# Two output accumulators in one PSUM bank, and the bank left over keeps a quarter of a V chunk

## The chip, the cores and the metric

The kernel runs on one core of a Trainium2 chip. Its time is the device time in microseconds (us), the median of several runs. A profile is one more execution, recorded by the hardware profiler, and it has its own time: the span from its first to its last instruction, and around the span a little that the span does not see.

The core has five engines, each with an instruction queue of its own that is worked off in order: TensorE (PE; its weight loads are shown as PEld), VectorE (DVE), ScalarE (ACT), GpSimd (POOL) and SyncE (SP), which here issues nearly all DMA transfers. SBUF is the working memory of 128 partitions. PSUM is the memory that TensorE writes its products to; it has eight banks, each 128 partitions by 512 float32.

## The reference, cut to what matters

The reference is two layers of decoding with one new position for each of 8 batch rows: attention over a cache, then a mixer with an MLP, and both once again. The caches are the same in both passes. (Lines are shortened; with a sequence of one position the shift brings in zeros alone, so `hs` is 0 and the kernel leaves it out.)

```python
B, Sq, D = 8, 1, 448
Hq, Hkv, Sk, Dh = 16, 8, 4096, 256        # k_cache, v_cache: (B, Hkv, Sk, Dh), bfloat16
...
def _A_ref(x, k_cache, v_cache, wq, wo):
    q = (x @ wq) split into Hq heads
    scores = einsum("bhqd,bhkd->bhqk", q, k) * (Dh ** -0.5)
    p = _softmax(scores, axis=-1)
    o = einsum("bhqk,bhkd->bhqd", p, v)
    return o as (B, Sq, Hq * Dh) @ wo

def _B_ref(x, w1, w2, w3, w4):
    hs = (h shifted along the sequence by quarters) @ w2   # h = _gelu(_layernorm(x) @ w1)
    x1 = x + hs
    return x1 + _gelu(_layernorm(x1) @ w3) @ w4
...
x = x + _A_ref(_layernorm(x, axis=-1), A_k_cache, A_v_cache, A_wq, A_wo)
x = x + _B_ref(_layernorm(x, axis=-1), B_w1, B_w2, B_w3, B_w4)
x = x + _A_ref(_layernorm(x, axis=-1), A_k_cache, A_v_cache, A_wq, A_wo)
x = x + _B_ref(_layernorm(x, axis=-1), B_w1, B_w2, B_w3, B_w4)
```

K and V of one batch row are 32 MiB together, 256 MiB for all rows, and each of the two attention passes needs all of them. What is computed per byte is little: two query heads share a K/V head.

## The kernel before

**Tiles.** The work of a row is cut into four pairs of K/V heads (`gp` 0 to 3). The K of a pair and the V of a pair are four *chunks* each, of 128 partitions x 8 KiB = 1 MiB. A chunk `c` of a pair is an *item* `(n, kv, c)`; `n` is the task (pass `ps`, row `b`, pair `gp`), `kv` is 0 for K and 1 for V. SBUF has 15 *places* of one chunk each (`slots`, `NC = 15`). Every item is loaded into a free place, used, and the place is given back.

**What stays between the passes.** Pass 1 of a row starts when pass 0 and the MLP of that row are done; meanwhile other rows' chunks are loaded. Eleven chunks of each row stay in their places from pass 0 to pass 1 and are not loaded again (`kept`: all K chunks of pairs 3 and 2, and V chunks 1 to 3 of pair 3). One more, `inner` (V chunk 1 of pair 2), stays in PSUM: `away` copies it with four transposes of 128x512 32-bit words into the four banks `store` (L719), and `back` copies it from there into a place before it is used in pass 1 (L726). A VectorE transpose turns blocks, and doing it twice gives the data back. So a row loads 52 of its 64 chunks from HBM.

**Order.** `items` fixes the order of work once and for all: the four K chunks of a task, with the V chunks of the task before it in between. The main loop takes one item after the other. After each item `emit_loads` issues every load for which a place is free, in the order of `loads`; all go through SP's one queue, so a load that waits for its place holds up those behind it. Two K chunks in neighbouring places can be loaded by one DMA of 2 MiB (L647). In the stretch in which a row's kept chunks lie in their places, only four of the 15 are left for the stream.

**A K chunk** is transposed in place by three VectorE instructions (`transpose_k`, L684), then TensorE makes scores into the bank `sc` (L699), ScalarE takes exponentials (L708), and the probabilities are transposed by TensorE (L735) and copied to `ptw` (L742). **A V chunk** takes 16 products of 128x256 (`pv`, L754), four in each quarter of the accumulator's partitions. Two pairs (a *half*, `g8`) add into one accumulator; there are two accumulators, `o_banks`, each in a PSUM bank of its own, of which the first 256 columns are used. The first four products of a half start the sums anew (`start=`, kept track of in `begun`), the others add.

**The end of a half** (`half`) is made in steps that the main loop spreads between items: VectorE takes the sums of exponentials (L398, L401), TensorE adds them up (L409), VectorE makes `rz` and `R` (L412, L429), ScalarE copies the accumulator to SBUF (L435) and the accumulator is free for the next half (`in_use`); at the next step TensorE multiplies the copy by `R` (L440) and VectorE casts the result (L444). This happens 31 times: 16 halves in pass 0, 15 in pass 1; the last row's first half of pass 1 is computed another way (`pv_cols`), in two of the `store` banks.

**PSUM.** The eight banks are `misc`, `sc`, two `o`, four `store`.

Of the kernel before, what the change touches and what calls it, by code (L numbers as in the profile page):

```python
# [8 lines left out]
FP32 = mybir.dt.float32  # L9
BF16 = mybir.dt.bfloat16  # L10
U32 = mybir.dt.uint32
# [6 lines left out]
def kernel(  # L18
# [27 lines left out]
    nc = tc.nc  # L46
# [3 lines left out]
    Dh = A_k_cache.shape[3]  # L50
# [5 lines left out]
    GP = G // 2  # L56
# [6 lines left out]
    kept = [(gp, 0, n) for gp in (GP - 1, GP - 2) for n in range(4)]  # L63
    kept += [(GP - 1, 1, n) for n in range(1, 4)]
    inner = (GP - 2, 1, 1)

    consts = ctx.enter_context(tc.tile_pool(name="consts", bufs=1))
    work = ctx.enter_context(tc.tile_pool(name="work", bufs=2))
    chn = ctx.enter_context(tc.tile_pool(name="chn", bufs=1))
    psum = ctx.enter_context(tc.tile_pool(name="psum", bufs=1, space=bass.MemoryType.PSUM))  # L70
# [4 lines left out]
    slots = [places_t[:, n * PB : (n + 1) * PB] for n in range(NC)]  # L75
# [32 lines left out]
    ptz = consts.tile([128, 520], BF16, name="ptw")  # L108
# [3 lines left out]
    misc = psum.tile([128, 512], FP32, name="misc")  # L112
    ot_bank = misc[:, 256:320]
    sc = psum.tile([128, 512], FP32, name="sc")
    o_banks = [psum.tile([128, 512], FP32, name=f"o{n}") for n in range(2)]
    store = [psum.tile([128, 512], FP32, name=f"store{n}") for n in range(4)]
    for t in [sc] + o_banks:
        nc.vector.memset(t[:], 0.0)

    def room_ps(what, nb):  # L120

# [301 lines left out]
    def half(o_ps, zall, g8, OT):  # L423


        rz = yield from z_cols(zall, range(2 * g8, 2 * g8 + 2))

        R = chn.tile([128, 8], FP32, tag="R")
        nc.vector.tensor_mul(  # L429
            R[:].rearrange("p (g n) -> p g n", n=4),  # L430
            rz[:].rearrange("p n g -> p g n"),
            fold[:].rearrange("p (g n) -> p g n", n=4),
        )
        o_sb = chn.tile([128, Dh], FP32, tag="o_sb")
        nc.scalar.copy(o_sb[:], o_ps[:, 0:Dh])  # L435
        in_use.remove(o_ps)
        yield
        ot_ps = ot_bank[:, 32 * g8 : 32 * g8 + 16].rearrange("p (j h) -> p j h", j=2)
        for j in range(2):
            nc.tensor.matmul(  # L440
                ot_ps[:, j], o_sb[:].rearrange("p (i j) -> p j i", j=2)[:, j], R[:], start=True, stop=True
            )
        yield
        nc.vector.tensor_copy(OT[:, :, 8 * g8 : 8 * g8 + 8], ot_ps)  # L444
        yield

    in_use = []
# [41 lines left out]
    def last(b, st):  # L489
        yield from half(st["o", 0], st["z"], 0, OT2[:, :, :, b])  # L490
# [13 lines left out]
    tasks = [(0, 0, gp) for gp in free + keep] + [(0, 1, gp) for gp in free]  # L504
# [26 lines left out]
    items, due = [], []  # L531
# [10 lines left out]
    def stays(it):  # L542
        n, kv, c = it
        return (tasks[n][2], kv, c) in kept

    def inside(it):
        n, kv, c = it
        return (tasks[n][2], kv, c) == inner

    loads = [it for it in items if not (tasks[it[0]][0] == 1 and (stays(it) or inside(it)))]  # L550

# [2 lines left out]
    where = {}  # L554
# [69 lines left out]
    def taken(it, p):  # L624

        where[it] = p
        n, kv, c = it
        if stays(it):
            where[tasks[n][1:], it[1:]] = p
        free_at[p] = again[tasks[n][1:], kv, c] if tasks[n][0] == 0 and stays(it) else used_at[it]  # L630

    def emit_loads(most=None):
        n = 0
        while loads and places and n != most:
            it = loads[0]
            both = both_for(it)
            if both:
                p, mate = both
                if p not in places or p + 1 not in places:
                    break  # L640
                for i, q in ((it, p), (mate, p + 1)):
                    loads.remove(i)
                    places.remove(q)
                    del held[i]
                    taken(i, q)
                _, b, gp = tasks[it[0]]
                nc.sync.dma_start(  # L647
                    places_t[:, p * PB : (p + 2) * PB],
                    A_k_cache[b, 2 * gp : 2 * gp + 2]
                    .rearrange("g s d -> (g s) d")  # L650
                    .rearrange("(p u z) d -> u p (z d)", u=2, z=32)[it[2] // 2],
                )
                n += 1
                continue
            p = place_for(it)
            if p is None:
                break
            del loads[0]
            taken(it, p)
            t, kv, c = it  # L660
            _, b, gp = tasks[t]
            dst = slots[p]
            rows = (A_v_cache if kv else A_k_cache)[b, 2 * gp : 2 * gp + 2].rearrange(
                "g s d -> (g s) d"
            )
            if kv:
                src = rows.rearrange("(a p y) d -> a p (y d)", a=4, y=16)[c]
            else:
                src = rows.rearrange("(p x y) d -> x p (y d)", x=4, y=16)[c]
            if loads:  # L670
                nc.sync.dma_start(dst[:], src)
            else:
                for y in range(2):
                    nc.sync.dma_start(
                        dst[:, 8 * Dh * y : 8 * Dh * (y + 1)], src[:, 8 * Dh * y : 8 * Dh * (y + 1)]
                    )
            n += 1
# [38 lines left out]
    def away(slot):  # L716

        for n in range(4):
            nc.vector.transpose(  # L719
                store[n][:].bitcast(U32), slot[:].bitcast(U32)[:, 512 * n : 512 * n + 512]  # L720
            )
# [22 lines left out]
            pt_ps.rearrange("p t k (a h) -> p a (t k) h", a=4),  # L744
        )

    def pv(o_ps, v, a, gp, begin):


        g = 2 * gp + a // 2  # L750
        for y in range(16):
            q = y % 4
            at = 128 * a + 8 * (4 * q + y // 4) + 6 - 2 * (g % 4)
            nc.tensor.matmul(  # L754
                o_ps[32 * q : 32 * q + 8, 0:256],
                ptz[:, at : at + 8],
                v[:, y * Dh : (y + 1) * Dh],
                start=(begin and y < 4),
                stop=(y >= 12),
                skip_group_check=True,  # L760
            )
# [39 lines left out]
            except StopIteration as e:  # L801
                return e.value

    gens, pairs_done, p_of, begun = [], {}, {}, set()

    def add_gen(kind, b, g, at, until, total):
        gens.append({"kind": kind, "b": b, "g": g, "at": at, "until": until, "n": 0, "of": total})
# [22 lines left out]
    for idx, it in enumerate(items):  # L830
# [7 lines left out]
        n, kv, c = it  # L838
        ps, b, gp = tasks[n]
# [5 lines left out]
        slot = slots[p]  # L845
        final = (ps, b) == (1, Bn - 1)
        if kv == 0:
# [6 lines left out]
            st = state[ps, b]  # L854
# [41 lines left out]
        else:  # L896
            st = state[ps, b]
# [5 lines left out]
            if final and gp in free:  # L903
                pv_cols(oc, slot, c, gp)
                if c % 2 == 1:

                    u = c // 2
                    scale_o(oc, rz_gp, gp, u, OT2[:, :, :, b])
                    h0 = 8 * gp + 4 * u
                    run(  # L910
                        add_cols(
                            st["y"],
                            lambda i: OT2[:, i % 2, i // 2, MID:],
                            wo_sb,
                            range(h0, h0 + 4),
                            4,
                            open=(claim(st), gp == free[-1] and u == 1),
                        )
                    )
            else:  # L920
                g8 = gp // 2
                if ("o", g8) not in st:
                    while len(in_use) == 2:
                        step(10 * len(items))
                    st["o", g8] = next(t for t in o_banks if all(t is not u for u in in_use))
                    in_use.append(st["o", g8])
                pv(st["o", g8], slot, c, gp, begin=(ps, b, g8) not in begun)
                begun.add((ps, b, g8))
                if ps == 0 and inside(it):
                    away(slot)  # L930
            if c == 3:
                done = pairs_done[ps, b] = pairs_done.get((ps, b), 0) + 1
                if done == 2 and ps == 0:
                    add_gen("chain", b, first_half(b, st), idx + 1, idx + (16 if b == 0 else 21), 10)
                elif done == 2:
                    add_gen("chain" if final else "last", b, first_last(b, st), idx + 1, idx + 13, 9)
                elif done == 4 and ps == 0:
                    add_gen("chain", b, chain(b, st), idx + 1, first_of[(1, b), 0] - 1, 38)
                elif done == 4 and not final:
                    add_gen("last", b, last(b, st), idx + 1, idx + (7 if b == Bn - 2 else 13), 6)  # L940
        if not (ps == 0 and stays(it)):
            if (ps, gp, kv, c) == (1, keep[-1], 0, 0):
                kept_place = p
            else:
                places.append(p)
        emit_loads()
        step(idx)
    while gens:
# [6 lines left out]
    for q in range(4):  # L955
        for fc in range(4):
            at = min(128 * fc, D - 128)
            lo, hi = max(W * q, 128 * fc), min(W * q + W, at + 128)
            if lo < hi:
# [4 lines left out]
                    start=(lo == W * q),  # L964
                    stop=False,
                    skip_group_check=True,
                )
    for c in range(HC):
        for q in range(4):
# [4 lines left out]
                start=False,  # L974
                stop=(c == HC - 1),
# [38 lines left out]
```

## Time and profile before

| | |
|---|---|
| median of 5 runs | 1104.07 us (1101.73 to 1109.72) |
| the profiled execution | 1105.06 us, of which the span is 1103.1 |
| TensorE busy / weight loads | 677.1 us (61%) / 453.0 us (41%) |
| VectorE busy | 586.3 us (53%) |
| ScalarE busy | 124.5 us (11%) |
| read from HBM | 446.77 MB, 405 GB/s over the span |
| granted TensorE clock, mean | 0.589 of full speed |

The page gives for each group of instructions its line, engine and operation, what it writes and reads, its count, then after the bar its busy time and the mean of one in ns, then the idle time of the engine before it and what ended most of that. The groups around the change:

```profile
L684 DVE STREAM_TRANSPOSE places<-places 128x512 uint32<-128x512 uint32 (+1 forms) x576 | 462.1, 858 | 279.6 <-DMA places<-in_A_k_cache_dram 276.5
...
L754 PE MATMUL o<-places,ptw 128*8 128x256 bf16 x3968 | 244.1, 390 | 138.1 <-DMA places<-in_A_v_cache_dram 128.7
```

VectorE's largest group waits for K chunks from HBM, and TensorE's products with V wait for V chunks. The section of DMA issues has line, number, size, and the median time from issue to landing:

```profile
places<-in_A_v_cache_dram SPq DMA_DIRECT2D x223, 1024.0 KB, 9.5
places<-in_A_k_cache_dram SPq DMA_DIRECT2D x146, 1024.0 KB, 10.3
places<-in_A_k_cache_dram SPq DMA_DIRECT2D x23, 2048.0 KB, 19.7
```

### The profile page before, as it was taken

What the parts mean: (1) busy time and instruction counts of PE and PEld (TensorE: products, weight loads), DVE (VectorE), ACT (ScalarE), POOL (GpSimd) and SP (SyncE); (2) the same over time, 40 slices, a digit from 0 to 9 for tenths busy, and PEclk for the clock granted to TensorE, in tenths of its full rate; (3) what the DMA queues carried; (4) which work ended last, traced back from release to release, by engine and by line L of the source; (5) the groups of instructions that cost most, each with busy time, mean ns of one, the idle gap of its engine ahead of it and who ended that gap; (6) DMA issues with size and microseconds to landing.
All of it is one profiled execution on the core that took longest, in us unless ns stands there. A gap on an engine that the chain in (4) does not pass through costs nothing. (4 is left out here: it accounts for less than half of the span.)

```text
span 1103.1 us, 32833 instructions
## 1 busy us (share of the span) xinstructions
PE 677.1 (61%) x15062; PEld 453.0 (41%) x15062; DVE 586.3 (53%) x1188; ACT 124.5 (11%) x362; POOL 16.3 (1%) x27
## 2 busy tenths in 40 slices
PE   3245677556864577446774467735776477767775
PEld 2123345334642355324542245523454244535554
DVE  4255564646356555455455564565637563575462
ACT  0001101110110011101011000201111101111110
POOL 0000000000000000000000000000000000000000
PEclk9996556655565556555566555765556555665575
DMA  9999999999999999999999999999999999999994
GB/s 359 395 425 420 419 403 416 419 412 406 416 423 421 394 390 424 423 418 388 419 420 424 420 398 419 423 422 417 411 416 421 419 405 420 420 411 404 414 418 182
DMA packets 62011, 448.90 MB, mean 407 GB/s; under 512 B 6569, under 2 KB 10545, under 8 KB 11313
## 3 DMA queue, kind: packets, MB, share of 16 engines
q1 hardware_dynamic: 61680, 446.42, 98.4%
q8 instruction: 118, 1.93, 0.7%
q10 hardware_dynamic: 192, 0.38, 0.1%
q14 instruction: 21, 0.16, 0.0%
HBM read 446.77 MB, written 0.01 MB: 405 GB/s over the span
## 5 line engine op out<-in xcount | busy, mean ns | idle before, releaser
L684 DVE STREAM_TRANSPOSE places<-places 128x512 uint32<-128x512 uint32 (+1 forms) x576 | 462.1, 858 | 279.6 <-DMA places<-in_A_k_cache_dram 276.5
L699 PE MATMUL sc<-places,qbd 128*8 128x128 bf16 (+1 forms) x6720 | 283.7, 310 | 227.6 <-DVE places L684 188.9
L754 PE MATMUL o<-places,ptw 128*8 128x256 bf16 x3968 | 244.1, 390 | 138.1 <-DMA places<-in_A_v_cache_dram 128.7
L699 PEld LDWEIGHTS <-qbd 128*8 128x8 bf16 x6720 | 162.8, 102 | 324.9 <-issue 148.1
L754 PEld LDWEIGHTS <-ptw 128*8 128x8 bf16 x3968 | 113.0, 110 | 185.1 <-issue 142.9
L708 ACT ACTIVATE p_n<-sc 128x256 bf16<-128x256 f32 x128 | 95.7, 748 | 808.1 <-PE sc L699 808.1
L287 PEld LDWEIGHTS <-wq_sb 128*128 128x128 bf16 x1152 | 36.0, 104 | 28.6 <-issue 18.9
L336 PEld LDWEIGHTS <-wo_sb 128*128 128x128 bf16 x1280 | 38.5, 102 | 19.6 <-issue 19.4
L310 DVE CAST qbd<-misc 32x64 bf16<-32x64 f32 x64 | 13.8, 216 | 61.3 <-PE misc L306 60.7
L287 PE MATMUL misc<-xb,wq_sb 128*128 128x1 bf16 x1024 | 34.6, 166 | 6.7 <-DVE xb L262 3.3
L336 PE MATMUL misc<-OT,wo_sb 128*128 128x1 bf16 x1024 | 34.4, 165 | 0.0
L708 ACT ACTIVATION_READ_ACCUMULATOR p_n<-sc 128x1 f32 x128 | 34.3, 268 | 0.0
L742 ACT CAST ptw<-misc 128x128 bf16<-128x128 f32 x64 | 17.5, 273 | 136.8 <-PE misc L735 76.7
L440 PEld LDWEIGHTS misc<-R,o_sb 128*128 128x128 f32 x124 | 27.1, 303 | 10.4 <-issue 8.3
L440 PE MATMUL misc<-R,o_sb 128*128 128x8 f32 x124 | 29.8, 351 | 0.4 <-ACT o_sb L435 0.3
L237 POOL TENSOR_TENSOR t<-t,nhalf 128x2 f32<-128x2 f32 (+2 forms) x20 | 14.0, 703 | 1073.6 <-DVE t L251 1073.6
L409 PE MATMUL misc<-zm,one 128*128 128x8 f32 (+1 forms) x66 | 18.3, 351 | 16.2 <-DVE zm L401 14.4
L726 DVE STREAM_TRANSPOSE places<-store 128x512 uint32<-128x512 uint32 x32 | 20.1, 685 | 11.3 <-PE sc L699 11.3
L409 PEld LDWEIGHTS misc<-zm,one 128*128 128x128 f32 x66 | 15.7, 296 | 22.4 <-issue 17.1
L354 PEld LDWEIGHTS <-w_sb 128*128 128x128 bf16 x560 | 17.2, 105 | 9.6 <-issue 9.4
L354 PE MATMUL misc<-xb,w_sb 128*128 128x1 bf16 (+1 forms) x560 | 18.4, 166 | 3.6 <-DVE xb L264 2.2
L719 DVE STREAM_TRANSPOSE store<-places 128x512 uint32<-128x512 uint32 x32 | 20.0, 694 | 1.0 <-DMA places<-in_A_v_cache_dram 0.9
(93 smaller groups left out, 227.2 us busy)
## 6 DMA issues: line engine op xcount, KB each, us to landing
places<-in_A_v_cache_dram SPq DMA_DIRECT2D x223, 1024.0 KB, 9.5
places<-in_A_k_cache_dram SPq DMA_DIRECT2D x146, 1024.0 KB, 10.3
places<-in_A_k_cache_dram SPq DMA_DIRECT2D x23, 2048.0 KB, 19.7
wo_sb<-in_A_wo_dram SPq DMA_DIRECT2D x1, 3584.0 KB, 27.0
wq_sb<-in_A_wq_dram SPq DMA_DIRECT2D x3, 1024.0 KB, 8.5
w_sb<-in_B_w_dram SPq DMA_DIRECT2D x1, 1568.0 KB
w_sb<-in_B_w_dram SPq DMA_DIRECT2D x3, 448.0 KB, 25.7
places<-in_A_v_cache_dram SPq DMA_DIRECT2D x2, 512.0 KB, 18.7
```

The source lines that it names most:

```text
L287: nc.tensor.matmul(q_ps[:, j * Hq + h, :], w, xbs(nb)[:, xi, :], start=(fc == 0), stop=(fc == 3),)
L336: nc.tensor.matmul(y_ps[:, fc, :], w[:, i, at : at + 128], rhs(i), start=start, stop=stop, skip_group_check=open is not None,)
L354: nc.tensor.matmul(h_ps[:, c * nb : c * nb + nb], w, xbs(nb)[:, xi, :], start=(fc == 0), stop=(fc == 3),)
L409: nc.tensor.matmul(z_ps, ones, zm[:], start=True, stop=True)
L440: nc.tensor.matmul(ot_ps[:, j], o_sb[:].rearrange("p (i j) -> p j i", j=2)[:, j], R[:], start=True, stop=True)
L684: nc.vector.transpose(w, w)
L699: nc.tensor.matmul(sc[32 * k : 32 * k + 8, 128 * x : 128 * (x + nx)], qbd[:, ep, gp].rearrange("p a h -> p (a h)"), v, start=(n == 0), sto ...
L708: nc.scalar.activation(p_sb[:, :, :, 2 * u : 2 * u + 2].rearrange("p t i x -> p x t i"), sc[:, 256 * u : 256 * u + 256].rearrange("p (x t ...
L719: nc.vector.transpose(store[n][:].bitcast(U32), slot[:].bitcast(U32)[:, 512 * n : 512 * n + 512])
L726: nc.vector.transpose(slot[:].bitcast(U32)[:, 512 * n : 512 * n + 512], store[n][:].bitcast(U32))
L742: nc.scalar.copy(ptw[:, :, :, 6:8], pt_ps.rearrange("p t k (a h) -> p a (t k) h", a=4),)
L754: nc.tensor.matmul(o_ps[32 * q : 32 * q + 8, 0:256], ptz[:, at : at + 8], v[:, y * Dh : (y + 1) * Dh], start=(begin and y < 4), stop=(y >= ...
```

## The change

The two accumulators become the two halves of one bank, `o_both`: columns 0 to 255 and 256 to 511. One TensorE product of zeros (128x512) at the start sets the whole bank; from then on no product starts a sum anew (`start=False`), and the half of the bank that ScalarE has just copied out is set to zero by VectorE (`memset`, 128x256), 31 times. `begun` goes.

The bank left over becomes `store[4]`. In pass 0, after the products with V chunk 0 of pair 3 (`part`), VectorE transposes the first quarter of that chunk (`Q4` = 4 x 256 columns, 128x512 32-bit words) into it. In pass 1 the load of this chunk brings only the other three quarters, 128 x 6 KiB, and VectorE transposes the first quarter from PSUM into the chunk's place. This instruction is issued at the end of the item just before the chunk's own. That is done once per row, 8 times. The number and the order of the loads stay as they are.

```diff
     inner = (GP - 2, 1, 1)
+    part = (GP - 1, 1, 0)
+    Q4 = 4 * Dh
...
-    o_banks = [psum.tile([128, 512], FP32, name=f"o{n}") for n in range(2)]
-    store = [psum.tile([128, 512], FP32, name=f"store{n}") for n in range(4)]
-    for t in [sc] + o_banks:
-        nc.vector.memset(t[:], 0.0)
+    o_both = psum.tile([128, 512], FP32, name="o")
+    o_banks = [o_both[:, 0:Dh], o_both[:, Dh : 2 * Dh]]
+    store = [psum.tile([128, 512], FP32, name=f"store{n}") for n in range(5)]
+    nc.vector.memset(sc[:], 0.0)
+    nc.tensor.matmul(o_both[:], ptz[:, 0:128], ptz[:, 0:512], start=True, stop=True)
...
-        nc.scalar.copy(o_sb[:], o_ps[:, 0:Dh])
-        in_use.remove(o_ps)
+        nc.scalar.copy(o_sb[:], o_ps)
+        nc.vector.memset(o_ps, 0.0)
+        in_use[:] = [t for t in in_use if t is not o_ps]
...
+    def halfway(it):
+        n, kv, c = it
+        return (tasks[n][2], kv, c) == part
...
-                nc.sync.dma_start(dst[:], src)
+                z0 = Q4 if tasks[t][0] == 1 and halfway(it) else 0
+                nc.sync.dma_start(dst[:, z0:], src[:, z0:])
...
-                o_ps[32 * q : 32 * q + 8, 0:256],
+                o_ps[32 * q : 32 * q + 8, :],
...
-                start=(begin and y < 4),
+                start=False,
...
+                if ps == 0 and halfway(it):
+                    nc.vector.transpose(store[4][:].bitcast(U32), slot[:, 0:Q4].bitcast(U32))
...
+        soon = items[idx + 1] if idx + 1 < len(items) else it
+        if tasks[soon[0]][0] == 1 and halfway(soon):
+            nc.vector.transpose(
+                slots[where[soon]][:, 0:Q4].bitcast(U32), store[4][:].bitcast(U32)
+            )
         emit_loads()
```

More of the change, by code (lines that the diff above doesn't have):

```diff
@@ L745, in transpose_p, with pv @@
         )
-    def pv(o_ps, v, a, gp, begin):
+    def pv(o_ps, v, a, gp):
         g = 2 * gp + a // 2
@@ L802, in run @@
                 return e.value
-    gens, pairs_done, p_of, begun = [], {}, {}, set()
+    gens, pairs_done, p_of = [], {}, {}
     def add_gen(kind, b, g, at, until, total):
@@ L926 @@
                     in_use.append(st["o", g8])
-                pv(st["o", g8], slot, c, gp, begin=(ps, b, g8) not in begun)
-                begun.add((ps, b, g8))
+                pv(st["o", g8], slot, c, gp)
                 if ps == 0 and inside(it):
                     away(slot)
+                if ps == 0 and halfway(it):
+                    nc.vector.transpose(store[4][:].bitcast(U32), slot[:, 0:Q4].bitcast(U32))
             if c == 3:
```

## The prediction

> **What bounds the kernel now.** I read the page's slices and queues first, then the table of windows, then the timeline of one slow stretch.
>
> ```profile
> span 1103.1 us, 32833 instructions
> ...
> DMA  9999999999999999999999999999999999999994
> GB/s 359 395 425 420 419 403 416 419 412 406 416 423 421 394 390 424 423 418 388 419 420 424 420 398 419 423 422 417 411 416 421 419 405 420 420 411 404 414 418 182
> ...
> q1 hardware_dynamic: 61680, 446.42, 98.4%
> ```
>
> The DMA engines are busy from the first slice to the last but one, and one queue carries the 446 MB. No compute engine is above 61%. In most slices the rate is 415 to 425 GB/s; in about one of four it falls to 388 to 406. Those dips decide whether saved bytes are saved time, so I look into one (columns: stretch, busy us per engine, TensorE clock, DMA share, GB/s):
>
> ```profile
> 505.00:510.00 5.00, 3.95 (x58) 2.68 (x59) 3.07 (x8) 0.54 (x2) 0.00 (x0) 0.50 0.93 359
> 510.00:515.00 5.00, 4.20 (x112) 2.94 (x111) 2.49 (x5) 0.74 (x2) 0.00 (x0) 0.50 0.99 352
> 515.00:520.00 5.00, 2.91 (x50) 1.68 (x51) 3.64 (x14) 0.00 (x0) 0.70 (x1) 0.50 0.96 382
> 620.00:625.00 5.00, 2.21 (x48) 1.26 (x48) 2.43 (x3) 0.75 (x2) 0.00 (x0) 0.50 1.02 426
> ```
>
> Then the timeline of that dip (start, us, engine, line):
>
> ```profile
> 506.41 0.38 ACT L435 COPY o_sb<-o 128x256 f32<-128x256 f32 x1
> 506.96 0.33 SPq L671 DMA_DIRECT2D places<-in_A_k_cache_dram  x1
> 507.37 1.02 PE L754 MATMUL o<-places,ptw 128*8 128x256 bf16 x16
> 507.72 0.17 DVE L429 TENSOR_TENSOR R<-rz,fold 128x8 f32<-128x8 f32 x1
> 508.45 0.33 SPq L671 DMA_DIRECT2D places<-in_A_v_cache_dram  x1
> 509.00 2.43 DVE L684 STREAM_TRANSPOSE places<-places 128x1024 uint32<-128x1024 uint32 x3 [1.10 <-DMA places<-in_A_k_cache_dram]
> 514.00 2.43 DVE L684 STREAM_TRANSPOSE places<-places 128x1024 uint32<-128x1024 uint32 x3 [2.51 <-DMA places<-in_A_k_cache_dram]
> 519.14 2.43 DVE L684 STREAM_TRANSPOSE places<-places 128x1024 uint32<-128x1024 uint32 x3 [0.47 <-DMA places<-in_A_k_cache_dram]
> ```
>
> VectorE starts each K chunk when it lands: at 509.00, 514.00, 519.14, then 524.44, one K and one V chunk apart, 5.15 us on average. In the undisturbed stretch the same rows start at 615.02, 620.11 and 625.11, 5.05 us apart. So the dip costs some 0.1 us per pair, not the 15% that its rate suggests: a chunk counts as landed when the slowest of 16 engines is done, and what idles here must be mostly engines that were ahead. The pace is set by the bytes in the queue, 2.5 us per MiB, nearly everywhere. The last V chunk has landed at 1090.2; the 13 us of tail behind it the change leaves alone.
>
> **The change, part by part.**
>
> *Fewer bytes.* Eight rows each load 128 x 6144 B instead of 128 x 8192 B. 8 x 262,144 B are 2.10 MB; at 420 GB/s that is 4.99 us. The packet records say nearly the same: 8192-byte packets take 311 ns (median), 4096-byte ones 159 ns, so a straight line gives 235 ns for 6144 B, 76 ns less. An engine gets 8 of the 128 packets of a load: 8 x 8 x 76 ns = 4.9 us. Bounds: 0, if the time of a packet does not fall with its size, and 5.0. I take **4.9**, since the 4096-byte row shows that it does fall.
>
> *Out to PSUM and back.* One transpose of 128x512 more in each direction and row. The rows of the existing kind:
>
> ```profile
> L719 DVE STREAM_TRANSPOSE store<-places x32: 682/684/727, 92.6 to 969.9; 128x512 uint32<-128x512 uint32 x32
> L726 DVE STREAM_TRANSPOSE places<-store x32: 674/674/718, 178.6 to 1045.0; 128x512 uint32<-128x512 uint32 x32
> L118 DVE MEMSET o<- x2: 485/485/485, 2.8 to 3.3; 128x512 f32 x2
> ```
>
> 8 x 0.69 + 8 x 0.68 = 11.0 us of VectorE, none of it on the path. The outward one waits for its V chunk, and behind it stand the transposes of the next K chunk, which lands 2.5 us after that V chunk. Counting the K chunks ahead of it, it falls in the full stretches (near 220, 353, 486, 618 us and so on), where VectorE sits idle 1.9 to 3.1 us before the next K chunk in seven of eight rows. Without that cover it would cost 8 x 0.69 = 5.5 us. It also joins what must end before the place is loaded again, but TensorE's 16 products on the same chunk hold the place for 1.0 us anyway. The backward one stands before the part chunk's products. In the row of 559 us it would start after the zeroing, at 561.0, and end at 561.7; VectorE is then idle until 564.70, and the next products on this accumulator start at 562.57. It waits only for the load of the place's previous tenant. Cost 0; bounds 0 and 8 x 0.68 = 5.4 us.
>
> *Zeroing, 31 times.* The trace has 128x512 at 485 ns and L837's 128x112 at 152 ns; the straight line between them gives 272 ns for 128x256, so 31 x 0.27 = 8.4 us of VectorE. Each stands behind R (L429) and waits for ScalarE's copy. Of the 31 copies 24 have ended before R ends. Seven end later: by 1.0 us at 428, 560, 691, 822 and 934, 2.2 at 295, 1.8 at 94. Queued behind on VectorE are K transposes or the small cast of L444; in the five and at 295 VectorE is idle for 3.7 to 6.2 us after R, at 94 about 0.1 us is left over. I take **0.1** in all; bounds 0 and 17.6 (8.4 plus the waits of 9.2), which would need VectorE to be the pace.
>
> *One bank.* In the changed program's order the first product after each zeroing waits for VectorE, also where it writes the other half, and 12 of the copies wait for products of the other half. The copies have cover: even after the latest of them ScalarE's next exponentials come 1.4 us later or more. The product has less. In the fence above L754 starts at 507.37, while R ends at 507.89, so zeroing ends at 508.17: the product is **0.80 us late**, and behind it on TensorE stand L440 and the next scores. Over the 31 I find 0.80 nine times, 0.35 five times, 1.5 once and 0.5 in three small ones: 11 us of waiting. Who waits for it: the place that this V chunk frees, and so the load that SP issues at 508.45, 0.06 us after the last product. Is that load needed so soon? The K load issued at 506.96 is used at 514.00, 7.04 us later, of which its own transfer is 2.5; so 4.5 us of start-up and older work lie before it, and I estimate that 2 to 3 us of that is queue. A delay of 0.80 fits in, and since the next landing does not move, it does not add up. TensorE itself idles 0.94 us before the next scores (timeline, at 510.29). Cost 0; bounds 0 and 11.
>
> Here the Trainium skill speaks against the change. "Perfetto Trace Analysis", section "Matmuls", says that independent groups should rotate through different banks, so that evacuation of one overlaps the products of the next; "PSUM — Partial Sum Buffer", section "PSUM bank collisions raise a hardware error", makes engines take turns per bank. The row of the copy is 0.40 us (31 rows, 12.3 us), so by the rule 31 x (0.40 + 0.27) = 20.8 us of products would stop being overlapped, and the sum would be +15.9 us. By the rows TensorE waits 11 us, while it is idle 39% of the span and the queue has work. I take the rows.
>
> *Start.* Two zeroings of 485 ns leave VectorE; one product of 128x512 comes before the transposition of x at 2.20 us, at most 0.7 us later. VectorE's copy of x stands at 4.49 behind its zeroings and moves up by up to 0.97. The q projection waits for wq until 10.05 in any case. Cost 0, bounds -0.5 and +0.5.
>
> **Sum.** -4.9 + 0.1 = -4.8 us. The span goes from 1103.1 to 1098.3, the profiled execution from 1105.06 to 1100.3. That execution is 1.0 us above the median of the five runs, 1104.07, so the median becomes **1099.3**, 0.43% faster. A measurement here tells about 0.5% (5.5 us) from no change, so the likeliest result lies just inside.
>
> **Rivals.**
> 1. *The queue is not the pace in the dips.* If places, not bytes, set the time there, the loads' saving is eaten by a later wait for a free place: about 1104 (1102 to 1105.5). For it: SP always waits for a place. Against it: 5.15 against 5.05 us per pair, and VectorE waits for K landings in and out of the dips.
> 2. *The shared bank costs more than the bytes save.* Place: the first product after a zeroing, in the dips. Price: 11 us, less 4.9, plus 0.1: +6.2, so 1110.3. It decides from the point where the queue's cover at those loads is under 0.8 us. For it: DMA share 0.93 at 505 to 510, just where such a delay falls. Against it: 7.04 us from issue to use.
> 3. *The smaller load saves nothing*, because 6144-byte packets run worse or the transfer is split differently: about 1104, with the page's DMA bytes down by 2.1 MB and the busy share unchanged.
>
> **How the numbers follow.** Forecast 0.72, its own range 1096 to 1102; its centre is 0.7 us short of the bound of 5.5, so I split it 0.34 faster and 0.38 same. Rivals 1 and 3 together 0.14: 0.12 same, 0.02 slower. Rival 2 has 0.12, all slower. 0.02 is left for a larger gain. That makes 0.36 faster, 0.50 same, 0.14 slower. The range of 8 in 10 reaches from the forecast's low end over rivals 1 and 3, and a little towards rival 2: 1096 to 1106.
>
> **What would show it.** Right: queue bytes 446.42 to 444.3 MB; rows of 8 + 8 transposes near 0.68 us and 31 zeroings near 0.27; K starts still about 5.05 us apart in the full stretches; TensorE waiting for the zeroing 11 us or less in all, with SP's issue at the place of 508.45 later by 0.8 and the following K start unmoved. Wrong: K starts in the dips 5.5 us or more apart, a longer wait of VectorE for the copy, or a DMA share below 0.9 in several windows.

## The result and the profile after

| | before | changed |
|---|---|---|
| median | 1103.22 us (79 runs, 1099.93 to 1113.44) | 1099.48 us (44 runs, 1094.86 to 1107.55) |
| ratio to before | | 0.9962, 95% interval 0.9951 to 0.9973 |
| span of the profiled execution | 1103.1 us | 1097.3 us |

The changed kernel is faster by 0.38%, 4.2 us of 1104 (3.0 to 5.4): a small gain, clear of zero, and less than the 0.5% that the prediction counted as a change that can be told from none. The prediction said -4.8 us and 1099.3.

First the page's slices and queues of the changed kernel:

```profile
span 1097.3 us, 32879 instructions
...
DMA  9999999999999999999999999999999999999994
GB/s 358 395 426 420 419 390 417 419 419 375 414 425 418 405 412 421 422 420 399 417 417 425 420 404 420 418 420 420 406 419 420 420 406 418 421 409 406 420 417 189
...
q1 hardware_dynamic: 61680, 444.32, 98.5%
```

The picture is that of before: one queue, busy to the last slice but one, 420 GB/s with a dip in about one slice of four. The queue carries 2.10 MB less. The costliest groups and the smaller load:

```profile
L693 DVE STREAM_TRANSPOSE places<-places 128x512 uint32<-128x512 uint32 (+1 forms) x576 | 462.1, 858 | 260.8 <-DMA places<-in_A_k_cache_dram 257.1
...
L763 PE MATMUL o<-places,ptw 128*8 128x256 bf16 x3968 | 241.0, 386 | 148.5 <-DMA places<-in_A_v_cache_dram 126.3
...
places<-in_A_v_cache_dram SPq DMA_DIRECT2D x8, 768.0 KB, 7.6
```

VectorE waits 19.4 us less for K chunks (276.5 before), about as much as it works more (603.5 us busy against 586.3). The idle time of TensorE ahead of the V products has risen from 138.1 to 148.5 us, while its part for V chunks has fallen by 2.4; most of the new part is the wait for the zeroing. The view of the accumulator's tile shows it (count, then ns of one as least/median/most; below them, us and times that an engine sat idle before a use of this tile, and what ended the wait):

```profile
L438 ACT COPY o_sb<-o x31: 372/378/422, 94.5 to 1060.1; 128x256 f32<-128x256 f32 x31
L439 DVE MEMSET o<- x31: 272/272/272, 95.0 to 1064.3; 128x256 f32 x31
...
  PE o L763: 33.6, 12
...
  ACT o_sb L438: 10.0, 7
  DVE o L439: 9.1, 11
...
  DVE t L224: 1.2, 5
```

ScalarE's copies waited 33.6 us for products (of the other half of the bank, in 12 of 31 cases), the zeroings 10.0 us for copies, and TensorE's products 9.1 us for zeroings, in 11 cases. The last line belongs to these waits. L224 is a small VectorE copy that stands right behind the zeroing in five cases; the profile names it, but the product starts as the zeroing ends (at 404, for one: zeroing from 404.06 to 404.33, product at 404.38). So products waited 10.3 us for zeroings, in 16 cases. And the transposes out and back:

```profile
L940 DVE STREAM_TRANSPOSE store<-places x8: 684/727/727, 108.0 to 973.8; 128x512 uint32<-128x512 uint32 x8
L958 DVE STREAM_TRANSPOSE places<-store x8: 675/683/719, 181.7 to 1042.0; 128x512 uint32<-128x512 uint32 x8
```

The timeline of the same dip that the prediction looked into (here some 1.6 us earlier):

```profile
505.42 0.33 SPq L680 DMA_DIRECT2D places<-in_A_k_cache_dram  x1
...
506.18 0.17 DVE L432 TENSOR_TENSOR R<-rz,fold 128x8 f32<-128x8 f32 x1
506.40 0.27 DVE L439 MEMSET o<- 128x256 f32 x1
506.72 1.03 PE L763 MATMUL o<-places,ptw 128*8 128x256 bf16 x16 [0.82 <-DVE o L439]
507.38 2.43 DVE L693 STREAM_TRANSPOSE places<-places 128x1024 uint32<-128x1024 uint32 x3 [0.71 <-DMA places<-in_A_k_cache_dram]
...
507.79 0.33 SPq L680 DMA_DIRECT2D places<-in_A_v_cache_dram  x1
508.68 0.98 PE L708 MATMUL sc<-places,qbd 128*8 128x128 bf16 x24
...
510.29 0.33 SPq L680 DMA_DIRECT2D places<-in_A_k_cache_dram  x1
...
512.32 2.43 DVE L693 STREAM_TRANSPOSE places<-places 128x1024 uint32<-128x1024 uint32 x3 [2.45 <-DMA places<-in_A_k_cache_dram]
...
517.26 2.43 DVE L693 STREAM_TRANSPOSE places<-places 128x1024 uint32<-128x1024 uint32 x3 [0.26 <-DMA places<-in_A_k_cache_dram]
...
522.20 2.43 DVE L693 STREAM_TRANSPOSE places<-places 128x1024 uint32<-128x1024 uint32 x3 [1.64 <-DMA places<-in_A_k_cache_dram]
```

The product has waited 0.82 us for the zeroing. The load for the place that it frees is issued at 507.79, 0.41 us after the K start at 507.38; before, that load came 0.55 us ahead of its K start (508.45 and 509.00). So it is 0.96 us later, and yet the next three K chunks are used 4.94 us apart each. The delay has been swallowed.

### The profile page after: what moved, and what is told of

Read it like the earlier page. It is cut to its first block, busy times and chain, and to the rows that moved or that the text cites. A ratio compares the mean times of both kernels' runs of the same rounds, so it can differ in the third digit from the quotient of the medians.

```text
span 1097.3 us, 32879 instructions
## 1 busy us (share of the span) xinstructions
PE 673.5 (61%) x15063; PEld 450.1 (41%) x15063; DVE 603.5 (55%) x1233; ACT 126.0 (11%) x362; POOL 16.3 (1%) x27
## 3 DMA queue, kind: packets, MB, share of 16 engines
q1 hardware_dynamic: 61680, 444.32, 98.5%
## 5 line engine op out<-in xcount | busy, mean ns | idle before, releaser
L708 PE MATMUL sc<-places,qbd 128*8 128x128 bf16 (+1 forms) x6720 | 280.6, 308 | 216.9 <-DVE places L693 178.7
L763 PE MATMUL o<-places,ptw 128*8 128x256 bf16 x3968 | 241.0, 386 | 148.5 <-DMA places<-in_A_v_cache_dram 126.3
L708 PEld LDWEIGHTS <-qbd 128*8 128x8 bf16 x6720 | 160.5, 101 | 311.4 <-issue 139.4
L412 PE MATMUL misc<-zm,one 128*128 128x8 f32 (+1 forms) x66 | 18.1, 348 | 16.4 <-DVE zm L404 15.9
L735 DVE STREAM_TRANSPOSE places<-store 128x512 uint32<-128x512 uint32 x32 | 20.1, 685 | 10.7 <-PE sc L708 10.6
L412 PEld LDWEIGHTS misc<-zm,one 128*128 128x128 f32 x66 | 15.5, 293 | 22.9 <-issue 16.9
```

What stands on the lines that cost most here:

```text
L412: nc.tensor.matmul(z_ps, ones, zm[:], start=True, stop=True)
L708: nc.tensor.matmul(sc[32 * k : 32 * k + 8, 128 * x : 128 * (x + nx)], qbd[:, ep, gp].rearrange("p a h -> p (a h)"), v, start=(n == 0), sto ...
L735: nc.vector.transpose(slot[:].bitcast(U32)[:, 512 * n : 512 * n + 512], store[n][:].bitcast(U32))
L763: nc.tensor.matmul(o_ps[32 * q : 32 * q + 8, :], ptz[:, at : at + 8], v[:, y * Dh : (y + 1) * Dh], start=False, stop=(y >= 12), skip_group ...
```

## The experiments

The first question was where the 4.2 us come from, and whether something of the change costs.

**Full load: the bank is shared, the quarter goes out, but pass 1 loads all of the part chunk.**

```diff
-                z0 = Q4 if tasks[t][0] == 1 and halfway(it) else 0
-                nc.sync.dma_start(dst[:, z0:], src[:, z0:])
+                nc.sync.dma_start(dst[:], src)
...
-        soon = items[idx + 1] if idx + 1 < len(items) else it
-        if tasks[soon[0]][0] == 1 and halfway(soon):
-            nc.vector.transpose(
-                slots[where[soon]][:, 0:Q4].bitcast(U32), store[4][:].bitcast(U32)
-            )
```

> The changed kernel with all of its costs and none of its bytes: the shared bank, the 31 zeroings and the transposes out to PSUM stay, but pass 1 loads the whole of V chunk 0 of pair 3, and the transposes back are left out. If the gain is the bytes and every cost is hidden: no change from the kernel before, ratio 1.000 (0.998 to 1.002), about 1103. If the shared bank costs something that the bytes had to pay back (rival 2, up to 11 us): 1.004 to 1.010.

Measured: ratio 0.9996 (0.9973 to 1.0019). With the bytes back the gain is gone, so the gain is the bytes. Of the costs of the shared bank, its zeroings and the transposes out nothing is seen, though the interval leaves room for 2 us.

**A quarter less: the kernel before, with only the bytes taken away** (`(1, GP - 1, 1, 0)` is pass 1, pair 3, V, chunk 0).

```diff
-                nc.sync.dma_start(dst[:], src)
+                z0 = 4 * Dh if (tasks[t][0], tasks[t][2], kv, c) == (1, GP - 1, 1, 0) else 0
+                nc.sync.dma_start(dst[:, z0:], src[:, z0:])
```

> The kernel before with the bytes alone taken away: in pass 1 the first quarter of V chunk 0 of pair 3 is not loaded (what lay in the place is used, so that part of the computation is left out); two banks, no zeroing, no transposes more. If all costs are hidden: the same time as the changed kernel, 4.9 us under the kernel before, ratio 0.9956 (0.994 to 0.997). If the change pays for its bytes in waits: clearly faster than the changed kernel, down to 0.990.

Measured: 0.9928 (0.9904 to 0.9951), 5.4 to 10.6 us less than before, and so more than the 4.9 us that the bytes are worth. I measured it once more, beside the changed kernel without its transposes:

> The kernel before with the first quarter of the part chunk not loaded in pass 1 (products of pass 1 read what was left there), measured once more beside the run without transposes. If the shared bank costs nothing, both have the same ratio; if the earlier 0.9928 was right and the bank costs 3 us or so, this one is 0.993 and the run without transposes 0.996.

> The changed kernel without its 16 transposes: the first quarter of the part chunk is neither put into PSUM nor brought back, and not loaded in pass 1 either, so the products of pass 1 read what an earlier chunk left in that quarter. The shared bank and its zeroings stay. If the transposes are covered, as I predicted: the ratio of the changed kernel, 0.996. If they are what separates the changed kernel (0.9962) from the kernel before with the same bytes left out (0.9928): about 0.993.

Its edit takes out both `nc.vector.transpose` calls of the change. Measured: 0.9953 (0.9938 to 0.9968) for the bytes alone (5.2 us, 3.5 to 6.8: what the bytes are worth), 0.9960 (0.9944 to 0.9977) with the shared bank, against 0.9962 with the transposes too. So the transposes cost nothing that can be seen (0.0002, with room for some 2 us). What the shared bank costs lies between nothing and about 3 us: the three comparisons put it at -0.4 (full load against 1), 0.8 (0.9960 against 0.9953) and, with the first run, up to 3.5 us. That is as far as these runs tell.

**Less in the dip, less in the full stretch.** Now the claim that bytes set the pace in the dips too. Three quarters of another V chunk are not loaded in pass 1: once one that lands in the dips, once one that lands where the rate is full. The edit is that of the last diff with `12 * Dh` and `(1, 1, 1, 2)` or `(1, 0, 1, 1)`.

> The kernel before with three quarters of one V chunk per row not loaded (what lay in the place is used), a chunk that lands in the middle of the dips (V chunk 2 of pair 1 in pass 1, landing near 517 in the row looked at). 8 x 0.75 MiB at 2.49 us per MiB are 14.9 us. If bytes set the pace in the dips too: ratio 0.9865 (0.985 to 0.989). If free places set the pace there (rival 1): far less, 0.995 to 1.000.

> The same three quarters less, but of a V chunk that lands in the full stretches (V chunk 1 of pair 0 in pass 1, landing near 582 in the row looked at). Both theories: 14.9 us less, ratio 0.9865 (0.985 to 0.989). It is the measure for the run with the chunk in the dips: equal if bytes set the pace everywhere, clearly faster than that one if places do in the dips.

Measured: in the dip 0.9978 (0.9962 to 0.9994), 2.4 us of the 14.9 that the bytes are worth, as free places would have it. In the full stretch 0.9940 (0.9918 to 0.9961), 6.6 us (4.3 to 9.1): more than in the dip, but less than half of what both theories expected. The slices of the run with less in the dip:

```profile
GB/s 357 395 424 421 415 394 420 419 419 375 409 423 420 390 408 421 422 421 380 411 420 425 421 378 416 423 422 418 378 401 421 421 404 418 422 415 373 404 418 192
```

The dips have become deeper: 380, 378, 378 and 373 where the kernel before had 388, 398, 411 and 404. Fewer bytes went through in the same time. Its timeline shows why (the load of 256 KB is the one issued at 505.87):

```profile
505.87 0.33 SPq L672 DMA_DIRECT2D places<-in_A_v_cache_dram  x1
506.42 2.43 DVE L685 STREAM_TRANSPOSE places<-places 128x1024 uint32<-128x1024 uint32 x3 [1.11 <-DMA places<-in_A_k_cache_dram]
...
509.33 0.33 SPq L672 DMA_DIRECT2D places<-in_A_k_cache_dram  x1
...
511.23 0.33 SPq L672 DMA_DIRECT2D places<-in_A_v_cache_dram  x1
511.36 2.43 DVE L685 STREAM_TRANSPOSE places<-places 128x1024 uint32<-128x1024 uint32 x3 [2.45 <-DMA places<-in_A_k_cache_dram]
...
514.27 0.33 SPq L672 DMA_DIRECT2D places<-in_A_k_cache_dram  x1
...
521.51 1.84 DVE L685 STREAM_TRANSPOSE places<-places 128x1024 uint32<-128x1024 uint32 x2 [2.26 <-DMA places<-in_A_k_cache_dram]
```

Compare SP's issues with those of the kernel before, reckoned from the same K start (506.42 here, 509.00 there): 2.91, 4.81 and 7.85 us behind it here; 2.91, 4.81 and 7.91 there (511.91, 513.81, 516.91). The small load frees the queue 1.9 us earlier, but SP issues no sooner, because it waits for a place, and a place comes free when the work on it ends: in both kernels the next K load goes out 2.91 us after a K start. Three K starts on, at 521.51, this kernel is 15.09 us from its 506.42; the one before is at 524.44, 15.44 us from 509.00. That is 0.35 us of 1.9, and not even this is clear: the changed kernel, which loads the chunk whole, takes 14.82 us there (507.38 to 522.20).

**One place fewer** (`NC = 15` becomes 14) asks the same from the other side.

> The changed kernel with 14 places instead of 15, so one place less for the stream in the dips. If the dips are paced by bytes with about one chunk (2.5 us) to spare: that is used up, 0 to 0.5 us lost per chunk in the dips, ratio 0.997 to 1.03. If places already set the pace at 15 (rival 1), a dip of some 60 us with three places for four grows by a third, 8 x 20 us: ratio above 1.10.

Measured: 1.0696 (1.0645 to 1.0746), 81 us above the changed kernel. Both expectations missed: it lies between them. Its slices:

```profile
GB/s 361 399 425 420 379 355 380 422 344 331 373 424 421 368 329 393 424 419 355 348 403 420 392 354 348 421 422 400 330 358 423 374 353 363 421 374 331 344 413 212
```

The full stretches stay at 419 to 425, and nearly all the loss is in the dips, down to 329. The same as a table: from the trace of each run I took when each chunk has landed (the last of its 16 DMA engines done), and from that the time between four fixed chunks of a row, mean of rows 1 to 4, in us. D is the stretch with the dips, and ends with the landing of the part chunk.

```
stretch (MiB before)    before  full load  changed  less in dip  less in full  5 zeroings  14 places
A part -> V3 pair 2  (7)  17.45    17.62     17.43      17.96        17.77        18.10      18.96
B -> K0 pair 1      (17)  42.77    42.84     42.85      42.49        41.06        42.82      42.34
C -> V0 pair 1       (9)  22.75    22.75     22.81      22.79        23.03        22.47      22.42
D -> next part      (19)  49.06    48.26     47.76      48.24        48.56        50.32      57.44
A to D                   132.03   131.47    130.85     131.48       130.42       133.71     141.16
```

In D, 0.75 MiB less took no time away (48.24 against 48.26 with the full load, the cleaner measure, since one row of the profiled execution before was 2 us late by itself). Seven of the rows say the same more closely: the short chunk and the eight loads behind it land in 23.1 us (mean), the same nine loads before in 23.1 and with the full load in 22.9. One place less put 9.7 us on (57.44 - 47.76).

In B, 0.75 MiB less took 1.8 us away, all that the bytes are worth; but 0.7 us of it came back in the other stretches (A to D: 131.47 - 130.42 = 1.05). Why some comes back I have not shown. The run is also less clean than its name: outside rows 1 to 4, in three places (at 244.6, 878.5 and 1011.3 us), a load close behind the short chunk lands 3.6 to 4.1 us after the one before it, as in the dips. So its 6.6 us are likely too low for the worth of bytes where the rate is full.

The part chunk's own quarter stands at the far end of D, beyond the dip. In the changed kernel this chunk lands 1.87 us after the one before it (median of 8 rows), with the full load 2.49: the quarter brings its whole 0.62 us. The total of D is too coarse for that: in the four runs without the quarter (changed, without transposes, twice a quarter less) it is 47.64 to 48.72.

**More zeroing.** Last the estimate of the cover: each zeroing was made 2, 3, 5, 9 and 17 times, so that the product behind it comes later by 0.27 us for each. The edit for five (the others have 2, 3, 9 or 17):

```diff
-        nc.vector.memset(o_ps, 0.0)
+        for _ in range(5):
+            nc.vector.memset(o_ps, 0.0)
```

> The changed kernel with each of the 31 zeroings done five times in a row, 4 x 0.27 = 1.1 us more each: the first product after it is 1.9 us late in the dips instead of 0.8. If the queue covers 2 to 3 us there: as the changed kernel, ratio to the kernel before 0.996 (0.995 to 0.999). If there is no cover and each late product is a late landing: 14 places in the dips x 1.1 = 15 us more, ratio about 1.010.

> Each zeroing done nine times, 2.2 us more: the product is 3.0 us late, which is the end of the cover that I estimate. Cover of 2 to 3 us: 0 to 10 us more than the changed kernel, ratio 0.996 to 1.005. No cover: 14 x 2.2 = 31 us more, about 1.024.

> Each zeroing done seventeen times, 4.35 us more: the product is 5.2 us late, past any cover that I see. Cover of 2 to 3 us: some 2 to 3 us at each of 14 places and more where K chunks wait behind the zeroing, 20 to 45 us more than the changed kernel, ratio 1.014 to 1.037. No cover: 61 us more, about 1.05. If even this is hidden, the queue is much deeper than I think: below 1.005.

> The changed kernel, but each of the 31 zeroings is made twice, so that the first product after it comes 0.27 us later than in the changed kernel (about 1.1 us later than in the kernel before, in the nine places where that was 0.8). Theory A, the dips are balanced and the cover ends between the 0.8 us of the changed kernel and the 1.9 us of the run with five zeroings, with a line of slope 1 behind it: five zeroings cost 21 us for 31 x 1.1 us, that is 62% of what was added; if the cover ends at the changed kernel itself, twice costs 31 x 0.27 x 0.62 = 5 us (ratio to before about 1.001); if cover is left, less: 0 to 2 us (0.996 to 0.998). The prediction's cover of 2 to 3 us: 0.996.

> The changed kernel, but each zeroing is made three times, 0.54 us more. No cover left: 31 x 0.54 x 0.62 = 10 us over the changed kernel, ratio to before about 1.006. Cover that ends near 1.4 us: 2 to 4 us, 0.998 to 1.000. The prediction's cover of 2 to 3 us: 0.996.

The waits are the products' waits for the zeroing, in the view of the accumulator's tile, with those that the profile puts down to the VectorE instruction right behind it: the copy L224, and from five zeroings on the transpose back, L959. The lines of two of these runs, three times and five times:

```profile
  DVE o L440: 20.2, 15
...
  DVE t L224: 5.2, 5
```

```profile
  DVE o L440: 33.0, 16
...
  DVE t L224: 9.2, 5
  DVE places L959: 3.0, 5
```

| zeroings | product waits, us | more than in the changed kernel | ratio to before (95%) | time over the changed kernel, us |
|---|---|---|---|---|
| 1 (the change) | 10.3 | | 0.9962 (0.9951 to 0.9973) | |
| 2 | 17.7 | 7.4 | 0.9985 (0.9963 to 1.0006) | 2.5 |
| 3 | 25.4 | 15.1 | 1.0031 (1.0013 to 1.0050) | 7.6 |
| 5 | 45.2 | 34.9 | 1.0151 (1.0102 to 1.0200) | 20.9 |
| 9 | 84.1 | 73.8 | 1.0312 (1.0261 to 1.0363) | 38.6 |
| 17 | 169.1 | 158.8 | 1.0905 (1.0843 to 1.0967) | 104.1 |

The last column is the difference of the ratios times 1104. The first 10 us of waiting cost 3.5 us at most (the comparisons above). The 2.5 us of two zeroings are not clear of zero; the 7.6 us of three are (about 5 to 10), half the length of the added wait. From there on a microsecond of waiting costs 0.5 to 0.8 us. So the cover ends close behind the change: its product is 0.8 us late in the dips; with two and three zeroings that makes 1.1 and 1.4.

With 5, 9 and 17 zeroings the time lies above even what was expected without any cover (1.010, 1.024 and 1.05). More products wait than the 14 reckoned with, and the dip with five zeroings shows what else is late:

```profile
510.91 0.33 SPq L681 DMA_DIRECT2D places<-in_A_k_cache_dram  x1
...
511.89 1.87 DVE L440 MEMSET o<- 128x256 f32 x5
513.67 2.40 DVE L694 STREAM_TRANSPOSE places<-places 128x1024 uint32<-128x1024 uint32 x3
513.82 1.03 PE L764 MATMUL o<-places,ptw 128*8 128x256 bf16 x16 [2.42 <-DVE o L440]
...
514.88 0.33 SPq L681 DMA_DIRECT2D places<-in_A_v_cache_dram  x1
...
515.73 1.02 PE L709 MATMUL sc<-places,qbd 128*8 128x128 bf16 x32
...
516.80 0.33 SPq L681 DMA_DIRECT2D places<-in_A_k_cache_dram  x1
...
517.81 2.43 DVE L694 STREAM_TRANSPOSE places<-places 128x1024 uint32<-128x1024 uint32 x3 [1.68 <-DMA places<-in_A_k_cache_dram]
...
523.90 2.43 DVE L694 STREAM_TRANSPOSE places<-places 128x1024 uint32<-128x1024 uint32 x3 [1.42 <-DMA places<-in_A_k_cache_dram]
```

The product waits 2.42 us, and the load behind it is issued 3.97 us after the K load (2.37 in the changed kernel: 505.42 and 507.79). But the K chunk, too, starts at 513.67 right behind the zeroings, 0.82 us after it landed. The K load at 516.80 goes out 0.05 us after the scores of that chunk end, and it is this load that is used late, at 523.90, 6.09 us after the one before it instead of 4.94. In the changed kernel VectorE still has 0.71 us to spare there between the zeroing and the K chunk. With three zeroings the room is just used up:

```profile
506.47 1.07 DVE L440 MEMSET o<- 128x256 f32 x3
507.49 2.43 DVE L694 STREAM_TRANSPOSE places<-places 128x1024 uint32<-128x1024 uint32 x3
```

TensorE has room of its own. In the kernel before it sits idle before the scores of this K chunk:

```profile
510.29 0.98 PE L699 MATMUL sc<-places,qbd 128*8 128x128 bf16 x24 [0.94 <-DVE places L684]
```

In the changed kernel the scores (508.68) follow the product with `R` without a gap: the late product has used this room up. Medians over the nine places where the product waits 0.82 us, in us:

```
zeroings                              1     2     3     5     9
K chunk starts after its landing     0.02  0.02  0.02  0.82  2.41
scores start after the K start       1.30  1.65  2.05  2.06  2.05
next K load after the K start        2.91  2.91  3.12  3.13  3.13
```

With three zeroings the next K load goes out 0.2 us later, because the scores are late; with five it is 1.0 us, of which VectorE makes 0.8. So the first three lines of the table of times price the wait of the product, and the last three price the wait of VectorE with it. How much of the 7.6 us comes by the scores, and how much by the late V load, these runs do not tell.

## Why the prediction was right, point by point

- **Fewer bytes, -4.9 us: right.** The 6144-byte packets took 234 ns (median of 1024) against 235 by the straight line, and the queue 444.32 MB. The full load showed that this is the whole gain. Measured 4.2 (3.0 to 5.4).
- **Out and back, cost 0: right.** 727 and 683 ns (0.69 and 0.68 said), and without them the ratio is the same.
- **Zeroing, 272 ns and a cost of 0.1 us: right.** The row has 272 ns, 31 times. VectorE's busy time rose by 17 us (603.5 against 586.3), and none of it can be found in the time.
- **One bank, 11 us of TensorE waiting, cost 0: the wait right, the reason for the zero too generous.** 10.3 us were measured, 0.82 in the dip. But the cover of 2 to 3 us was mis-sized. It would have hidden three zeroings (1.4 us) altogether, and they cost 7.6 us. The cover is used up somewhere from 0.8 us (the change) to 1.4 (three zeroings). The queue itself may be as long as I estimated: the shortest time from issue to landing of any run is 4.62 us (17 zeroings), so of the 7.04 us 2.4 were more than a load needs. (The K load issued at 509.33 in the run with less in the dip landed 5.67 us after its issue; by that it would be 1.4.) What ran out first is room on the engines: TensorE's 0.94 us before the scores, which the prediction named beside the queue, is spent by the change itself, and VectorE's last 0.71 us are spent by three zeroings. Rival 2 was to decide from a cover under 0.8 us. It did not, by a few tenths of a microsecond.
- **The rule of the Trainium skill on rotating banks** ("Perfetto Trace Analysis", section "Matmuls"), by which the sum would have been +15.9 us, was rightly set aside for a wait of this size: the full load, with all of the sharing and none of the saving, stood at 0.9996. A wait of this kind does cost time once it is a little longer: with three zeroings 7.6 us.
- **The bound, "The pace is set by the bytes in the queue, 2.5 us per MiB, nearly everywhere", meant of the dips too: wrong in the dips.** There the places set it: 0.75 MiB less per row bought nothing, a place less cost 9.7 us per row. I had read the pitch of 5.15 us against 5.05 as the sign that bytes rule; it only says that in this kernel the two limits lie within a few per cent of each other. The forecast held because the saved quarter lands behind the dip, where bytes do count (1.87 us for this chunk instead of 2.49). The prediction did not ask where it lands, so that much of its success was luck. Rival 1 had the mechanism of the dips, not its place.
- **Start, 0**: the product of zeros took 0.61 us at 2.2 us, and no run tells its cost apart from the rest.

A version that keeps still more was not tried: all eight banks are in use.

## What to carry to other kernels

A pitch that equals the transfer time does not prove that the transfers set it: take bytes away in that very stretch, and see whether the rate stays and the time falls, or the time stays and the rate falls. What a saved transfer brings depends on where in the stream it stands, so look at the stretch it lands in, not at the mean. And hidden waits should be dosed: a wait that costs nothing may be tenths of a microsecond from costing half its length, which only a run with two or three times the wait shows. Then look at every engine that the longer wait holds up, or a second delay is priced as the first.

## What was unexpected of the hardware

- A chunk's 16 DMA engines do not finish together. In the profiled executions the last was done 1.7 to 3.4 us after the first (10th and 90th percentile; median 2.7 before, 2.4 changed), about as long as a whole chunk takes back to back (2.49 us). The landing is the last one's, so a DMA share near 1 goes with 352 to 383 GB/s in the dips without telling which limit holds.
- A 1 MiB load whose bytes take 2.49 us in a full queue landed no sooner than 4.62 us after its issue in any run (17 zeroings), and no sooner than 4.75 with 14 places; in the changed kernel the shortest was 6.75. If the bytes took 2.49 us in that load too, at most 2.1 us of it were start-up and completion; the rest of the 6.75 is waiting in the queue.
